# Where the rest tokens' transposed q stands in SyncE's queue, and four dummy matmuls less in the opening

## The chip, the cores and the metric

The kernel runs on one core of one Trainium2 chip. The metric is the device time of one execution in microseconds (us), lower is better. Eight runs of the kernel before took 285.57 to 286.43 us, with a median of 286.01 us.

## The reference

A linear attention is followed by a two-layer feed-forward network with a tanh gelu. The shapes are 8 batches, 8 heads, 576 tokens and 64 dimensions per head; the attention's result is read as 4608 tokens of 512 features, and the hidden layer has 2048.

```python
def phi(x):
    return np.where(x > 0, x, np.exp(x) - 1.0) + 1.0
q_p, k_p = phi(q), phi(k)
kv  = np.einsum('bhsd,bhse->bhde', k_p, v)
z   = np.sum(k_p, axis=2)
num = np.einsum('bhsd,bhde->bhse', q_p, kv)
den = np.einsum('bhsd,bhd->bhs', q_p, z)[..., None] + 1e-06
x   = (num / den).transpose(0, 2, 1, 3).reshape(B * S, H * D)
h   = x @ w_in
g   = 0.5 * h * (1 + tanh(sqrt(2/pi) * (h + 0.044715 * h**3)))
out = g @ w_out
```

## The kernel before, in words

**Tiling.** Of each batch's 576 tokens, 512 are its main part, in four chunks of 128. The last 64 of two batches together make one more tile of 128, the "rest" tile m of batches 2m and 2m+1. The network (`iteration(j)`, L736) is run for j = 0 to 7 on the 512 main tokens of batch j, and for j = 8 on the four rest tiles. An iteration is a list of steps that TensorE runs in order: 16 steps "h" (four matmuls of 128x512 each, L380, then a gelu on ScalarE, L390), and after them the steps "o" (four matmuls of 128x512 each, L720). After each step, `run(j, slot)` calls what was planned for this slot with `at(j, slot, fn, ...)` (L498): the preparation and the attention of the batches to come are written into these slots by hand. Each engine takes its instructions in the order in which they were written.

**The attention of a batch.** phi(x) is computed as min(exp(x), max(x + 1, 1)): the exponential on ScalarE (`exp_of`, L218), the linear part on VectorE (`linear_of`, L226), and the minimum on VectorE (`least_of`, L232). Then q's phi has to be transposed, so that it can be the weights of the matmuls with kv. From batch 2 on this is done by DMA transposes that SyncE issues: `least_q(b)` (L595) computes the minimum for q and issues one DMA transpose per chunk, for chunks 0, 1, 2 and 3 (L599). The rest tile has the same steps in `plan_rest(m)` (L668): its exponential at slot 15 of iteration m+2, and at slot 22 its linear part, its minimum and one DMA transpose into `qtr` (L673).

**Order around the change.** From batch 4 on, `plan_attention(b)` (L634) writes the attention of batch b into iteration j = b-1. At slot 4, that is after five h steps, `early` (L644) runs on TensorE 32 small matmuls with chunks 1 and 0 of the transposed q, then 16 with the rest tile's `qtr` (L282, m = b-4), and then the h steps go on. VectorE divides (L294, L295), and SyncE transposes the three results (L622, L649). At slot 22, `late` (L652) does chunks 2 and 3, the kv of the next batch (L248), and calls `least_q(b+1)`. In the same slot 22, after `late`, the `least` of `plan_rest` runs. So in SyncE's queue, in iterations 3 to 5, the four transposes of batch b+1's q come first and the transpose of the rest tile m = b-3 comes fifth; all five are used from slot 4 of the next iteration on, where the order of use is: chunks 1 and 0, the rest tile, and from slot 22 on chunks 2 and 3. In iteration 2, rest tile 0 has slot 22 to itself. SyncE's queue also carries all loads, and the transposes of the attention's results.

**The opening.** `first_batch` (L407) prepares batch 0. The function `keep_warm(n)` (L410) puts n matmuls of 128x512 on zeros into TensorE's queue, whose result nothing reads: 18 at the start, 10 after the first half of q is transposed on TensorE (L422), 7 after the second half, then one between the two groups of kv matmuls (L248). The first of these groups takes the first half of k and of v, the second takes the second half. v is cast to bf16 by VectorE in two halves (L237), k's phi is computed by VectorE just before. Each group's result is copied into `kvbd` by VectorE and ScalarE (L260), and the first matmuls with q follow (L353, L264).

Of the kernel before, what the change touches and what calls it, by code (L numbers as in the profile page):

```python
# [9 lines left out]
BF16 = mybir.dt.bfloat16  # L10
# [5 lines left out]
def kernel(  # L16
# [15 lines left out]
    nc = tc.nc  # L32
# [3 lines left out]
    P = 128  # L36
    HP = P // 2
    C = 4
    MAIN = P * C
    REST = S - MAIN  # L40
    NP = H // 2
# [12 lines left out]
    pt = ctx.enter_context(tc.tile_pool(name="pt", bufs=2))  # L54
# [3 lines left out]
    psm = ctx.enter_context(tc.tile_pool(name="psm", bufs=2))  # L58
# [17 lines left out]
    def bank(name, shape, dt=FP32):  # L76
        return ps_b.tile(shape, dt, name=name, tag="b")

    def pair_of_banks(name):
        return ps_a.tile([P, 2, 512], FP32, name=name, tag="a")  # L80
# [115 lines left out]
    phi, exps = {}, {}  # L196

    def maps_view(name, b, x, out, hs):


        i = x[:, hs].rearrange("p h (c d) -> p h c d", d=D)
        o = out[:, :, hs, :].rearrange("p c h d -> p h c d")
        if name == "qr" or (name == "q" and b > 1):
            i = i.rearrange("p (u a) c d -> p a u c d", a=2)
            o = o.rearrange("p (a u) c d -> p a u c d", a=2)
        return o, i

    def phi_tiles(name, b):
        n, hn = ld[name, b].shape[2] // D, ld[name, b].shape[1]
        phi[name, b] = pphi.tile([P, n, hn, D], BF16, name=name + "_p")  # L210

    def exp_of(name, b, hs=None):
        x = ld[name, b]
        hs = hs or slice(0, x.shape[1])
        if (name, b) not in exps:
            exps[name, b] = pe.tile([P, x.shape[2] // D, x.shape[1], D], BF16, name=name + "_e")
        o, i = maps_view(name, b, x, exps[name, b], hs)
        nc.scalar.activation(o, i, AF.Exp)  # L218

    def linear_of(name, b, hs=None):  # L220
        x = ld[name, b]
        hs = hs or slice(0, x.shape[1])
        if (name, b) not in phi:
            phi_tiles(name, b)
        o, i = maps_view(name, b, x, phi[name, b], hs)
        nc.vector.tensor_scalar(o, i, 1.0, 1.0, op0=ALU.add, op1=ALU.max)  # L226

    def least_of(name, b, hs=None):
        p, e = phi[name, b], exps[name, b]
        if hs:  # L230
            p, e = p[:, :, hs, :], e[:, :, hs, :]
        nc.vector.tensor_tensor(p, p, e, op=ALU.min)  # L232
# [69 lines left out]
    def x_tile():  # L302
        return px.tile([P, d_model], BF16, name="x")
# [72 lines left out]
    qts = {}  # L376
# [30 lines left out]
    def first_batch():  # L407
        w_ps = bank("w_ps", [P, 512])

        def keep_warm(n):  # L410
            for _ in range(n):
                nc.tensor.matmul(w_ps, lhsT=warm[:, 0:P], rhs=warm)  # L412

        qt = pt.tile([P, C, NP, P], BF16, name="qt")
        qs = (slice(0, 4), slice(4, 8))

        def transpose_q(s, fn):
            t_ps = bank("t_ps", [P, C, 2, P], BF16)
            for i in range(2):
                for c in range(C):  # L420
                    h = 4 * s + 2 * i
                    nc.tensor.transpose(  # L422
                        t_ps[:, c, i, :], phi["q", 0][:, c, h : h + 2, :], ident
                    )
            fn(out=qt[:, :, 2 * s : 2 * s + 2, :], in_=t_ps)

        keep_warm(18)
        for s in range(2):
            for n, hs in (("q", qs[s]), ("k", halves[s])):
                exp_of(n, 0, hs)  # L430
                linear_of(n, 0, hs)
                least_of(n, 0, hs)
        transpose_q(0, nc.scalar.copy)
        keep_warm(10)
        transpose_q(1, nc.scalar.copy)
        keep_warm(7)
        for ii in range(2):
            cast_v_paired(0, halves[ii], nc.vector.tensor_copy)
        kv_ps = [bank("kv_ps", [P, E]) for _ in range(2)]
        kv_paired(0, 0, lambda a, ii: kv_ps[a])  # L440
        for a, fn in enumerate((nc.vector.tensor_copy, nc.scalar.copy)):
            kv_evac(0, slice(2 * a, 2 * a + 1), kv_ps[a].rearrange("p (i e) -> p i e", i=1), fn)
        keep_warm(1)
        kv_ps = pair_of_banks("kv_ps")
        kv_paired(0, 1, lambda a, ii: kv_ps[:, a, 0:E])
        kv_evac(0, slice(1, 4, 2), kv_ps[:, :, 0:E], nc.vector.tensor_copy, nc.scalar.copy)
        for fs in (slice(0, 128), slice(128, 256), slice(256, 512)):
            cast_w_in(0, nc.gpsimd.tensor_copy, fs)
        cast_w_in(1, nc.gpsimd.tensor_copy, slice(256, 512))
        for i in range(2, 4):  # L450
            cast_w_in(i, nc.gpsimd.tensor_copy)
        for i in range(2):
            cast_w_out(i, nc.gpsimd.tensor_copy)

        xts[0] = pt.tile([P, NP, MAIN], BF16, name="xt")
        x = {0: x_tile()}

        def t(c, blocks=range(NP)):
            transpose_x(x[c], xt_chunk(0, c), nc.scalar.copy, blocks)

        def h(m, c, blocks=range(KM)):
            h_begin(0, m, slice(P * c, P * (c + 1)), blocks)

        first, second = range(2), range(2, 4)
        nab_half(x[0], qt[:, 0], 0)
        nab_half(x[0], qt[:, 0], 1)
        x[1] = nab(qt[:, 1], 0)
        t(0, first)
        h_begun[0][0] = bank("h_ps", [P, MAIN])
        nc.tensor.matmul(h_begun[0][0], lhsT=warm[:, 0:P], rhs=warm, skip_group_check=True)  # L470
        t(0, second)
        for m in range(2):
            h(m, 0, first)
        x[2] = nab_in_banks(qt[:, 2], 0)
        h(0, 0, second)
        t(1)
        h(1, 0, second)
        x[3] = nab(qt[:, 3], 0)
        cast_w_in(1, nc.vector.tensor_copy, slice(0, 256))
        h(2, 0)  # L480
        h(3, 0)
        t(2)
        for m in range(3):
            h(m, 1)
        t(3)
        gelu_table()
        h(3, 1)
        for c in (2, 3):
            for m in range(4):
                h(m, c)  # L490
# [7 lines left out]
    def at(j, slot, fn, *args):  # L498


        fill.setdefault((j, slot), []).append((fn, args))
# [90 lines left out]
        else:  # L592
            at(j, s + 2, least_of, "k", b)

    def least_q(b):  # L595
        least_of("q", b)
        qts[b] = pt.tile([P, C, NP, P], BF16, name="qt")
        for c in range(C):
            nc.sync.dma_start_transpose(  # L599
                out=qts[b][:, c],  # L600
                in_=phi["q", b][:, c].rearrange("p h d -> p (h d)"),
            )

    def kv_in_pair(b):
        kv_ps = pair_of_banks("kv_ps")
# [18 lines left out]
    rest_qt = {}  # L624
# [9 lines left out]
    def plan_attention(b):  # L634


        j, m = b - 1, b - 4

        def pair_of_chunks(c):
            in_banks = nab_quads_in_banks(qts[b][:, c + 1], (b, b))  # L640
            in_pair = nab_quads(qts[b][:, c], (b, b))
            return (c + 1, in_banks), (c, in_pair)

        def early():  # L644
            chunks = pair_of_chunks(0)
            rest = nab_quads_in_banks(rest_qt[m], (2 * m, 2 * m + 1))
            transposed_x(b, 1, chunks[0][1]())
            x = rest()
            nc.sync.dma_start_transpose(out=xt_rest[:, :, P * m : P * (m + 1)], in_=x)  # L649
            transposed_x(b, 0, chunks[1][1]())  # L650

        def late():  # L652
            chunks = pair_of_chunks(2)
            if b + 1 < B:
                kv_ps = [bank("kv_ps", [P, 2, E]) for _ in range(2)]
                for ii in range(2):
                    kv_paired(b + 1, ii, lambda a, ii: kv_ps[a][:, ii, :])
            for c, x_of in chunks:
                transposed_x(b, c, x_of())
            if b + 1 < B:  # L660
                for a in range(2):
                    nc.vector.tensor_copy(out=kvs[(b + 1) % 4][:, 2 * a : 2 * a + 2, :], in_=kv_ps[a])
                least_q(b + 1)

        at(j, 4, early)
        at(j, 22, late)

    def plan_rest(m):  # L668
        def least():
            linear_of("qr", m)  # L670
            least_of("qr", m)
            rest_qt[m] = psm.tile([P, NP, P], BF16, name="qtr")
            nc.sync.dma_start_transpose(  # L673
                out=rest_qt[m], in_=phi["qr", m][:, 0].rearrange("p h d -> p (h d)")
            )

        at(m + 2, 15, exp_of, "qr", m)
        at(m + 2, 22, least)

    def evac(dst, src, on_scalar):  # L680
        (nc.scalar.copy if on_scalar else nc.vector.tensor_copy)(dst, src)  # L681
# [105 lines left out]
    for b in range(4, B):  # L787
        plan_prepare(b, (b - 2, 13), (b - 2, 15))
        plan_attention(b)
        plan_rest(b - 4)  # L790
    for b in range(6, B):
        at(b - 3, 6, load_rest, b - 4)
        at(b - 3, 6, load_batch, b)
# [35 lines left out]
```

## Time and profile before

| quantity | value |
|---|---|
| median of 8 runs | 286.01 us (285.57 to 286.43) |
| the profiled execution, its own time | 285.72 us |
| its span, first to last instruction | 283.9 us, so 1.8 us lie outside |
| TensorE (PE) busy | 275.8 us, 97% |
| ScalarE (ACT) busy | 161.9 us, 57% |
| VectorE (DVE) busy | 106.0 us, 37% |
| weight loads (PEld) busy | 135.9 us, 48%, beside the matmuls |
| GpSimd (POOL) busy | 15.5 us, 5%, all before 43 us |
| 590 matmuls of L720, 551 of L380 | 126.2 us and 114.4 us |
| 35 recorded dummy matmuls of L412 (36 issued) | 10.6 us |
| DMA transposes of q by chunks (L599), issue to landing | 24, median 2.6 us |
| DMA transposes of a rest tile's q (L673), issue to landing | 4, 2.4 to 3.5 us |

All times inside the execution are in us from the start of the span. PE stands for a matmul on TensorE, PEld for a weight load, SPq for SyncE's queue of DMA issues, and L282 for line 282 of the code. In a timeline, a row has a start, the time from the start of its first to the end of its last instruction, the engine, the line, the operation with what it writes and reads, and how many instructions are merged into the row; in brackets stands how long the engine was idle before it, and for whom. Matmuls overlap one another: one of 128x512 has a length of 379 ns in the records, while the next begins 216 ns after it. So the time that work takes on TensorE is best read from start to start.

### The profile page before, as it was taken

The page shows a single profiled execution, that of the slowest core. Times are in us where ns is not written, and L with a number is a line of the kernel's source. Part 1 is how long each engine was busy: PE and PEld are TensorE (multiplying, and loading weights), DVE is VectorE, ACT ScalarE, POOL GpSimd, SP SyncE. Part 2 cuts the span into 40 slices and gives each one's busy share as a digit, 9 for nine tenths or more (in the row PEclk, how much of TensorE's full clock was granted, in tenths as well). Part 3 has the DMA queues.
Part 4 walks back from the last instruction along what each step waited for, and adds up shares of the span by engine and source line. Part 5 has one row for each costly group of instructions (what it writes and reads, how often), then busy time and mean ns, then how long its engine had stood idle before and what let it go on. Part 6 is the DMA issues. An engine that isn't in the chain of part 4 may idle for free.

```text
span 283.9 us, 5380 instructions
## 1 busy us (share of the span) xinstructions
PE 275.8 (97%) x2263; PEld 135.9 (48%) x2297; DVE 106.0 (37%) x193; ACT 161.9 (57%) x222; POOL 15.5 (5%) x22
## 2 busy tenths in 40 slices
PE   8999999999999999999999999999999999999995
PEld 3584455445454444445444544454444444444444
DVE  3850376344956342727080808081403000000001
ACT  4678878776966925693568445872650165027400
POOL 4147210000000000000000000000000000000000
PEclk9999999999999999999999999999999999999999
DMA  7999999968699868997539874015300510120022
GB/s 247 400 407 396 411 401 404 404 232 221 74 233 339 229 166 236 283 370 242 150 79 341 265 169 42 17 49 164 106 19 15 126 46 0 61 88 1 0 74 76
DMA packets 59591, 53.83 MB, mean 190 GB/s; under 512 B 35760, under 2 KB 45360, under 8 KB 59568
## 3 DMA queue, kind: packets, MB, share of 16 engines
q1 hardware_dynamic: 56784, 44.58, 52.9%
q10 hardware_dynamic: 2784, 8.91, 8.5%
q8 instruction: 18, 0.29, 0.4%
q14 instruction: 5, 0.04, 0.0%
HBM read 36.70 MB, written 9.44 MB: 163 GB/s over the span
## 4 chain that ended last, share of the span: by engine, by line
PE 94%; SPq 2%; DMA 1%; issue 1%; DVE 1%; ACT 0%
PE h_ps L380 42%; PE o_ps L720 42%; PE w_ps L412 4%; PE kv_ps L248 2%; SPq L599 2%; PE n_ps L282 1%; DMA qtr<-qr_p 1%; PE n_ps L264 1%; PE t_ps L372 1%; PE t_ps L526 0%; PE t_ps L422 0%; DVE x L362 0%; DVE kvbd L260 0%; DVE o_sb L681 0%; PE n_ps L353 0%
## 5 line engine op out<-in xcount | busy, mean ns | idle before, releaser
L720 PE MATMUL o_ps<-w_out_sb,g 128*128 128x512 bf16 (+2 forms) x590 | 126.2, 367 | 1.4 <-issue 0.6
L380 PE MATMUL h_ps<-xt,w_in_sb 128*128 128x512 bf16 (+1 forms) x551 | 114.4, 359 | 0.8 <-issue 0.2
L390 ACT ACTIVATE g<-h_ps 128x512 bf16<-128x512 f32 x144 | 84.9, 598 | 42.1 <-PE h_ps L380 40.3
L720 PEld LDWEIGHTS <-g 128*128 128x128 bf16 x608 | 57.4, 98 | 64.0
L380 PEld LDWEIGHTS <-w_in_sb 128*128 128x128 bf16 x628 | 57.9, 98 | 62.8
L681 ACT COPY o_sb<-o_ps 128x512 f32<-128x512 f32 (+1 forms) x19 | 10.8, 576 | 64.0 <-PE o_ps L720 62.4
L681 DVE COPY o_sb<-o_ps 128x512 f32<-128x512 f32 (+1 forms) x19 | 12.2, 648 | 72.4 <-PE o_ps L720 72.4
L295 DVE TENSOR_TENSOR x<-n_ps,r 128x256 bf16<-128x256 f32 (+1 forms) x49 | 26.4, 539 | 1.7
L294 DVE RECIPROCAL r<-n_ps 128x4 f32<-128x4 f32 (+1 forms) x49 | 9.2, 187 | 36.2 <-PE n_ps L282 26.6
L232 DVE TENSOR_TENSOR k_p<-k_p,k_e 128x2304 bf16<-128x2304 bf16 (+1 forms) x9 | 11.0, 1223 | 22.1 <-ACT k_e L218 21.8
L218 ACT ACTIVATE k_e<-k_x 128x2304 bf16<-128x2304 f32 (+1 forms) x9 | 17.1, 1903 | 0.8 <-DMA k_x<-in_k_dram 0.8
L218 ACT ACTIVATE q_e<-q_x 128x2048 bf16<-128x2048 f32 (+1 forms) x9 | 15.4, 1715 | 2.8 <-DMA q_x<-in_q_dram 2.8
L226 DVE TENSOR_SCALAR q_p<-q_x 128x2048 bf16<-128x2048 f32 (+1 forms) x9 | 9.9, 1103 | 13.2 <-DMA q_x<-in_q_dram 13.2
L232 DVE TENSOR_TENSOR q_p<-q_p,q_e 128x2048 bf16<-128x2048 bf16 (+1 forms) x9 | 9.9, 1102 | 11.5 <-ACT q_e L218 11.4
L380 PE MATMUL h_ps<-xt_rest,w_in_sb 128*128 128x512 bf16 x63 | 13.9, 379 | 0.1
L226 DVE TENSOR_SCALAR k_p<-k_x 128x2304 bf16<-128x2304 f32 (+1 forms) x9 | 11.0, 1220 | 4.2 <-DMA k_x<-in_k_dram 4.2
L412 PE MATMUL w_ps<-warm 128*128 128x512 bf16 x35 | 10.6, 454 | 1.2 <-DVE warm L181 1.2
L237 DVE CAST vp<-v_x 128x2304 bf16<-128x2304 f32 (+1 forms) x9 | 11.0, 1225 | 1.8 <-DMA v_x<-in_v_dram 1.6
L403 ACT ACT_TABLE_LOAD x8 | 10.3, 1283 | 0.1
L218 ACT ACT_TABLE_LOAD x7 | 9.0, 1283 | 0.1
L141 POOL CAST w_in_sb<-w_st 128x512 bf16<-128x512 f32 (+2 forms) x6 | 7.6, 1269 | 14.2 <-DMA w_st<-in_moe_w_in_dram 14.2
L412 PEld LDWEIGHTS <-warm 128*128 128x128 bf16 x36 | 3.9, 113 | 6.3 <-issue 2.9
(45 smaller groups left out, 77.2 us busy)
## 6 DMA issues: line engine op xcount, KB each, us to landing
out_dram<-o_sb ACTq DMA_DIRECT2D x16, 512.0 KB, 3.7
k_x<-in_k_dram SPq DMA_DIRECT2D x7, 1152.0 KB, 9.4
v_x<-in_v_dram SPq DMA_DIRECT2D x7, 1152.0 KB, 11.6
q_x<-in_q_dram SPq DMA_DIRECT2D x6, 1024.0 KB, 7.9
w_st<-in_moe_w_in_dram SPq DMA_DIRECT2D x3, 1024.0 KB, 13.4
q_x<-in_q_dram SPq DMA_DIRECT2D x4, 512.0 KB, 8.3
w_st<-in_moe_w_out_dram SPq DMA_DIRECT2D x2, 1024.0 KB, 12.5
w_st<-in_moe_w_out_dram SPq DMA_DIRECT2D x4, 512.0 KB, 11.2
```

The costliest lines, as they stand in the source:

```text
L218: nc.scalar.activation(o, i, AF.Exp)
L226: nc.vector.tensor_scalar(o, i, 1.0, 1.0, op0=ALU.add, op1=ALU.max)
L232: nc.vector.tensor_tensor(p, p, e, op=ALU.min)
L237: fn(out=vp_paired(b)[:, :, us, 0:D].rearrange("p j u d -> p u j d"), in_=ld["v", b][:, us].rearrange("p u (j d) -> p u j d", d=D),)
L294: nc.vector.reciprocal(r, n_v[heads + (D,)])
L295: nc.vector.tensor_tensor(x_v, n_v[heads + (slice(0, D),)], r[heads + (None,)].to_broadcast(shape + [D]), op=ALU.mult,)
L380: nc.tensor.matmul(h_ps[:, ts], lhsT=w_in_sb[:, c, P * m : P * (m + 1)], rhs=xt[:, c, ts], start=(c == 0), stop=(c == KM - 1), skip_group_ ...
L390: nc.scalar.activation(g[:, m, :], h_ps, AF.Gelu_apprx_tanh)
L403: nc.scalar.preload_act_table_set("gelu_apprx_tanh_and_others")
L412: nc.tensor.matmul(w_ps, lhsT=warm[:, 0:P], rhs=warm)
L681: (nc.scalar.copy if on_scalar else nc.vector.tensor_copy)(dst, src)
L720: nc.tensor.matmul(o_ps, lhsT=g[:, m, P * t : P * (t + 1)], rhs=w_out_sb[:, m, fs], start=(m == 0), stop=(m == MM - 1),)
```

## The change

Two things are changed.

In iterations 3 to 5, the rest tile's linear part, minimum and DMA transpose are called from inside `least_q`, between the transposes of q's chunks 0 and 1 and those of chunks 2 and 3. SyncE's queue then holds chunk 0, chunk 1, rest, chunk 2, chunk 3, where it held chunk 0, 1, 2, 3, rest. VectorE's order of instructions is what it was: q's minimum, then the rest tile's linear part and minimum. ScalarE's and GpSimd's orders are also the same, and so is the slot of everything. Iteration 2 keeps its rest tile 0 at slot 22.

In the opening, the dummy matmuls after the two transposes of q are 8 and 5, where they were 10 and 7.

```diff
         transpose_q(0, nc.scalar.copy)
-        keep_warm(10)
+        keep_warm(8)
         transpose_q(1, nc.scalar.copy)
-        keep_warm(7)
+        keep_warm(5)
...
-    def least_q(b):
-        least_of("q", b)
-        qts[b] = pt.tile([P, C, NP, P], BF16, name="qt")
-        for c in range(C):
+    def transposed_q(b, cs):
+        for c in cs:
             nc.sync.dma_start_transpose(
                 out=qts[b][:, c],
                 in_=phi["q", b][:, c].rearrange("p h d -> p (h d)"),
             )
+
+    def least_q(b, m=None):
+
+        least_of("q", b)
+        qts[b] = pt.tile([P, C, NP, P], BF16, name="qt")
+        transposed_q(b, (0, 1))
+        if m is not None:
+            least_rest(m)
+        transposed_q(b, (2, 3))
...
-                least_q(b + 1)
+                least_q(b + 1, b - 3)
...
-    def plan_rest(m):
-        def least():
-            linear_of("qr", m)
-            least_of("qr", m)
-            rest_qt[m] = psm.tile([P, NP, P], BF16, name="qtr")
-            nc.sync.dma_start_transpose(
-                out=rest_qt[m], in_=phi["qr", m][:, 0].rearrange("p h d -> p (h d)")
-            )
-
-        at(m + 2, 15, exp_of, "qr", m)
-        at(m + 2, 22, least)
+    def least_rest(m):
+        linear_of("qr", m)
+        least_of("qr", m)
+        rest_qt[m] = psm.tile([P, NP, P], BF16, name="qtr")
+        nc.sync.dma_start_transpose(
+            out=rest_qt[m], in_=phi["qr", m][:, 0].rearrange("p h d -> p (h d)")
+        )
...
     for b in range(4, B):
         plan_prepare(b, (b - 2, 13), (b - 2, 15))
         plan_attention(b)
-        plan_rest(b - 4)
+        at(b - 2, 15, exp_of, "qr", b - 4)
+    at(2, 22, least_rest, 0)
```

## The prediction

> **What bounds the kernel now.** I read the busy shares first and then the chain that ended last.
>
> ```profile
> PE 275.8 (97%) x2263; PEld 135.9 (48%) x2297; DVE 106.0 (37%) x193; ACT 161.9 (57%) x222; POOL 15.5 (5%) x22
> ...
> PE 94%; SPq 2%; DMA 1%; issue 1%; DVE 1%; ACT 0%
> ```
>
> TensorE is busy 97% of the span and carries 94% of the chain. So only two things can shorten this kernel: work taken off TensorE where nothing else is late, and a wait of TensorE that goes. The chain names one place where it leaves TensorE for SyncE's queue and a DMA. Told in order of time (start, length, what):
>
> ```profile
> 158.65 4.28 PE o_ps L720 x19
> 162.93 1.03 SPq L599
> ...
> 167.94 0.02 SPq L673
> ...
> 167.99 3.47 DMA qtr<-qr_p
> 171.46 0.04 issue
> 171.51 0.32 PE n_ps L282 x16
> ```
>
> Iteration 4 ends, SyncE issues q's four transposes one after the other, then the rest tile's; that one lands 3.47 us later, and TensorE's 16 matmuls with it start at 171.51. How much this costs I read not from the idle time in brackets, but from start to start, because matmuls overlap. TensorE's timeline at the four places where a rest tile is used:
>
> ```profile
> 111.58 0.45 PE L282 MATMUL n_ps<-kv,qt 64*64 64x65 bf16 x32
> 111.87 0.32 PE L282 MATMUL n_ps<-kvbd,qtr 64*64 64x65 bf16 x16
> ...
> 141.01 0.45 PE L282 MATMUL n_ps<-kv,qt 64*64 64x65 bf16 x32
> 141.47 0.32 PE L282 MATMUL n_ps<-kvbd,qtr 64*64 64x65 bf16 x16
> ...
> 170.62 0.45 PE L282 MATMUL n_ps<-kv,qt 64*64 64x65 bf16 x32
> 171.51 0.32 PE L282 MATMUL n_ps<-kv,qtr 64*64 64x65 bf16 x16 [0.44 <-DMA qtr<-qr_p]
> ...
> 200.65 0.45 PE L282 MATMUL n_ps<-kv,qt 64*64 64x65 bf16 x32
> 200.93 0.32 PE L282 MATMUL n_ps<-kv,qtr 64*64 64x65 bf16 x16
> ```
>
> From the 32 matmuls with q to the 16 with the rest tile it is 0.29 us at the first place and 0.28 us at the fourth, where nothing is waited for. At the third it is 0.89 us, so 0.61 us are lost. At the second it is 0.46 us, so 0.18 us are lost, though no bracket says so. The fourth is close: its transpose was issued at 197.86 and took 2.9 us, so it landed at about 200.76, some 0.14 us before its first weight load at 200.90.
>
> **Part one: the rest tile third in the queue instead of fifth.** It removes and adds no instruction. It moves one DMA transpose ahead of two others, in each of iterations 3 to 5. Two issues of q's transposes take about 2 x 1.26 = 2.5 us in SyncE's timeline (162.71 for the first, 5.18 us for all four), so at the third place the rest tile is issued at about 165.2 and, even with the same 3.5 us, lands at 168.7. The 16 matmuls could have begun at 170.90. That is 2.2 us to spare, and it covers the 0.61 us four times over. Its data is ready: VectorE ends the rest tile's minimum at 162.17 (161.74 + 0.43), before the first of q's transposes is issued at 162.71. So the transposes of chunks 2 and 3, which now stand behind it, wait for no VectorE either; they are one issue of 1.2 to 1.7 us later, and they are first used in slot 22, at 187.47, some 15 us after landing. Behind the five transposes stands the transpose of an attention result, which waits for VectorE's division (issued at 172.24) and doesn't move for this. What would be late next are chunks 1 and 0 of q, which TensorE needs at 170.62; they keep their places and were issued by 165.2, so they have over 2 us too. Gain: 0.61 + 0.18 = **0.79 us** in this execution. Bounds: in a run whose transposes land a little sooner, 0.2 us; in one where all three land 0.3 us later than here, about 1.5 us (0.91 + 0.48 + 0.16).
>
> The page DMA: Bandwidth & Descriptors of the Trainium skill, in Latency and other measured facts, gives DMA transposes 261 GB/s; for 128x512 values of 2 bytes I estimate 0.50 us each from it. By that figure, passing two transposes would be worth 1.0 us and not 2.5 us, which still covers the whole wait; the trace's rows (1.26 us per issue, 2.3 to 5.7 us to landing) disagree with it as a time per transpose, and they decide.
>
> **Part two: four dummies less.** A dummy costs 216 ns from start to start once TensorE is up to speed: the first of ten starts at 7.69, and what follows them at 9.85. Two fewer twice is 4 x 0.216 = 0.86 us of TensorE's queue. What counts is what waits for TensorE there:
>
> ```profile
> 9.85 0.61 PE L422 MATMUL t_ps<-ident,q_p 128*128 128x128 bf16 x8
> ...
> 10.76 0.76 DVE L237 CAST vp<-v_x 128x1152 bf16<-128x1152 f32 x1
> 11.63 0.76 DVE L237 CAST vp<-v_x 128x1152 bf16<-128x1152 f32 x1
> ...
> 11.90 0.48 PE L248 MATMUL kv_ps<-vp,k_p 64*64 64x65 bf16 x36
> 12.31 0.39 PE L412 MATMUL w_ps<-warm 128*128 128x512 bf16 x1
> 12.63 0.37 PEld L248 LDWEIGHTS <-k_p 64*64 64x64 bf16 x36 [0.23 <-issue]
> ...
> 13.18 0.29 DVE L260 CAST kvbd<-kv_ps 64x130 bf16<-64x130 f32 x1 [0.21 <-PE kv_ps L248]
> ```
>
> The second transposes could start 0.43 us sooner, at 9.42; VectorE has their input at 9.31 (8.62 + 0.69). The five dummies then end at about 11.05. The first kv group needs the first cast, done at 11.52, and can start at about 11.57 instead of 11.90; it takes 0.41 us, the one dummy after it 0.32 us to the next group, so TensorE would be ready for the second group at 12.30. But this one needs the second cast, done at 12.39: it starts at about 12.44 instead of 12.63. From here VectorE, which runs without a break from 7.83 to 12.39, is the bound, so 0.86 us of dummies bring **0.19 us**. The copies into `kvbd`, the first matmuls with q and the divisions follow in a chain and move with it. Is it kept? Things that do not move with TensorE have to be in time: the last quarter of the first part of w_in is cast on GpSimd by 15.45 and used after 16.24; batch 1's v is cast by 39.54 (38.18 + 1.36) and used at 39.87, the least spare I found, 0.33 us. So 0.19 us are kept. Bounds: 0 if a load is later than here, 0.86 us if TensorE and not VectorE is late in the opening.
>
> That last bound isn't idle. The dummies' weight loads are 0.43 us apart until 5.43 and 0.22 us from 5.73 on, although the granted clock reads 1.00 throughout: TensorE starts at half speed. The page TensorE: Matmul & The Clock Gate of the Trainium skill, Part 1, says that the clock opens after about 3.4 us of activity in a window that runs freely, so that the moment differs from run to run, and that an idle window of that length closes it. By that rule the sum above stands, or grows in a run that warms up later; no row of one trace can show the spread.
>
> **Sum.** 285.72 - 0.79 - 0.19 = 284.74 us for the profiled execution. It lies 0.29 us below the median of the runs shown, 286.01; taking the same 0.98 us off the median gives 285.0 us.
>
> **Rivals.**
> 1. *The opening gives nothing back*, because a load or VectorE holds the second kv group or a later cast. For it: the spare of 0.33 us at 39.87 is small. Against it: 0.19 fits in. Time: 286.01 - 0.79 = 285.2.
> 2. *The rest tile's wait was mostly this execution's.* For it: two of four places have no wait at all, and landing times range from 2.4 to 3.5 us. Against it: three of the four places lie within 0.2 us of a wait or in one, and the median run is slower than the profiled one. With 0.2 us from each part: 285.6.
> 3. *More than forecast*: TensorE warms up later in the usual run, so that the dummies are late there and removing them is worth up to 0.86 us. Time: 286.01 - 0.79 - 0.86 = 284.4.
> 4. *Slower*: the clock falls in the opening. Place: after the second dummies, TensorE now idles from 11.05 to 11.57, 0.52 us, and two idle stretches of about 0.4 us (before 13.81 and 14.82) follow. It decides from the point at which these add up to too little activity. Price: at the start the half speed lasted from 1.19 to 5.73, 4.5 us; as long a fall, in TensorE's work after 14 us, costs half of it, 2.3 us. Time: 286.01 - 0.79 + 2.3 = 287.5. Against it: with the two stretches of 0.4 us there now, the eight matmuls of 128x128 at 16.41 still take 0.45 us, 56 ns each, which is full speed.
>
> That the change doesn't do what it says is excluded: the order of the queues shows chunk 0, 1, rest, 2, 3 in iterations 3 to 5 and four dummies less.
>
> **How the numbers follow.** Forecast 0.52 (284.7 to 285.4), rival 1 0.15, rival 2 0.13, rival 3 0.11, rival 4 0.09. The range from 284.4 to 285.75 reaches over rivals 1 and 2 and to rival 3, and leaves out rival 4 and the edges of the others, below 2 in 10. About 0.2% (0.57 us) is what a measurement of this kernel can tell from no change, so faster means under 285.44: the forecast and rival 1 nearly whole, and rival 3, 0.75; the same is rival 2 and an edge of the forecast, 0.16; slower is rival 4, 0.09.
>
> **What would show it.** In the profile after: at all four places 0.28 to 0.29 us from the matmuls with q to those with the rest tile, and no SPq or qtr in the chain; the second kv group at about 12.4 and the copy into `kvbd` on VectorE at about 13.0; TensorE idle before the first kv group, with VectorE's cast named as its releaser; the matmuls at about 16.2 still 56 ns apart. It would be wrong if a wait stood in front of chunks 1 and 0 at slot 4, if matmuls of 128x128 after 13 us were 110 ns apart, or if TensorE waited for a cast near 39.7.

## The result, and the profile after

The changed kernel takes 284.71 us (median of 15 runs, 284.63 to 284.89). The kernel before, run beside it and before it, takes 285.71 us (median of 41 runs, 284.88 to 286.75). The ratio is 0.9964, with a 95% interval of 0.9955 to 0.9973: 0.36% faster, 1.0 us. Beside the median the spread changed: 0.26 us now, 1.87 us before.

The profiled execution took 284.64 us, with a span of 282.9 us. Its busy shares and the shares of its chain:

```profile
PE 274.9 (97%) x2260; PEld 135.7 (48%) x2293; DVE 105.9 (37%) x193; ACT 162.0 (57%) x222; POOL 15.5 (5%) x22
...
PE 93%; DMA 3%; issue 1%; SPq 1%; DVE 1%; ACT 0%
```

TensorE is busy for the same share as before. But the DMA in the chain is another one. Before, it was the rest tile's transpose at 168 us. Now it is the load of v's second half in the opening (chain in order of time: start, length, what):

```profile
3.36 8.18 DMA v_x<-in_v_dram
...
11.56 0.77 DVE vp L237
...
12.38 0.52 PE kv_ps L248 x33
```

The half lands at 11.54, VectorE casts it until 12.33, and only then TensorE's second kv group starts. The dummies, which stood here before, are gone from the chain. From here to the end the chain is TensorE, with a few short steps of VectorE and ScalarE in the opening and one at the end.

At the two places where TensorE had waited for the rest tile, the timeline now reads:

```profile
140.75 0.45 PE L282 MATMUL n_ps<-kv,qt 64*64 64x65 bf16 x32
141.03 0.32 PE L282 MATMUL n_ps<-kvbd,qtr 64*64 64x65 bf16 x16
...
170.18 0.45 PE L282 MATMUL n_ps<-kv,qt 64*64 64x65 bf16 x32
170.46 0.32 PE L282 MATMUL n_ps<-kv,qtr 64*64 64x65 bf16 x16
```

From start to start it is 0.28 us at both, as at the other two places (0.29 and 0.28). It was 0.46 and 0.89. So 0.18 + 0.61 = 0.79 us are gone. The queues around the second place (SPq is SyncE's, ACTq ScalarE's):

```profile
162.17 2.52 SPq L597 DMA_TRANSPOSE qt<-q_p  x2
164.78 1.22 SPq L679 DMA_TRANSPOSE qtr<-qr_p  x1
166.05 3.03 SPq L597 DMA_TRANSPOSE qt<-q_p  x2
166.58 0.39 ACTq L712 DMA_DIRECT2D out_dram<-o_sb  x1
```

The rest tile's transpose (L679, the old L673) stands third and landed 2.3 us after its issue, at 167.1, more than 3 us before it is needed. Note the last row: ScalarE issues a store of 512 KB 1.8 us after it. In the profile before, this store was issued 0.97 us *ahead* of the rest tile's transpose, which then took 3.5 us:

```profile
167.02 0.35 ACTq L709 DMA_DIRECT2D out_dram<-o_sb  x1
167.99 1.64 SPq L673 DMA_TRANSPOSE qtr<-qr_p  x1
```

This neighbour, which the prediction did not weigh, is what e4, e5 and e11 are about.

The opening:

```profile
10.69 1.63 DVE L237 CAST vp<-v_x 128x1152 bf16<-128x1152 f32 x2
11.50 0.37 PEld L248 LDWEIGHTS <-k_p 64*64 64x64 bf16 x36 [0.61 <-DVE vp L237]
...
12.38 0.48 PE L248 MATMUL kv_ps<-vp,k_p 64*64 64x65 bf16 x36 [0.40 <-DVE vp L237]
```

Both kv groups now wait for VectorE's cast, as the brackets say. The second starts 0.25 us sooner than before (12.63), and 0.07 us of this is not the change's: the loads came a little sooner, so that VectorE's second cast ends at 12.32 instead of 12.39. That leaves 0.18 us. The two terms add to 0.79 + 0.18 + 0.07 = 1.04 us, against 1.08 us between the two profiled executions (285.72 and 284.64).

### The profile page after: what moved, and what is told of

Its sections match the earlier page's. It is cut to its first block, busy times and chain, and to the rows that moved or that the text cites. A ratio compares the mean times of both kernels' runs of the same rounds, so it can differ in the third digit from the quotient of the medians.

```text
span 282.9 us, 5373 instructions
## 1 busy us (share of the span) xinstructions
PE 274.9 (97%) x2260; PEld 135.7 (48%) x2293; DVE 105.9 (37%) x193; ACT 162.0 (57%) x222; POOL 15.5 (5%) x22
## 4 chain that ended last, share of the span: by engine, by line
PE 93%; DMA 3%; issue 1%; SPq 1%; DVE 1%; ACT 0%
PE h_ps L380 44%; PE o_ps L723 44%; DMA v_x<-in_v_dram 3%; PE kv_ps L248 2%; PE n_ps L282 1%; PE n_ps L264 1%; PE t_ps L372 1%; SPq L92 1%; SPq L97 0%; PE t_ps L526 0%; DVE vp L237 0%; DVE x L362 0%; DVE kvbd L260 0%; DVE o_sb L684 0%; PE n_ps L353 0%
## 5 line engine op out<-in xcount | busy, mean ns | idle before, releaser
L412 PE MATMUL w_ps<-warm 128*128 128x512 bf16 x31 | 9.6, 474 | 1.2 <-DVE warm L181 1.2
L248 PE MATMUL kv_ps<-vp,k_p 64*64 64x65 bf16 x576 | 6.6, 194 | 0.5 <-DVE vp L237 0.4
## 6 DMA issues: line engine op xcount, KB each, us to landing
w_st<-in_moe_w_out_dram SPq DMA_DIRECT2D x2, 1024.0 KB, 12.5
```

Of the source, the lines that this page charges most:

```text
L248: nc.tensor.matmul(kv_of(a, ii)[HP * s : HP * (s + 1)], lhsT=kp[r, j, u, :], rhs=vp[r, j, u, :], start=(j == 0), stop=(j == J - 1), skip_g ...
```

## The experiments

Two theories stood against each other at first: that there are two gains, most of it from the rest tile's wait, or that most of it comes from the opening. Later the question became what makes the wait so long. Kernels e1 to e4 ran on one chip, e5 to e8 on a second, e9 to e12 on a third; each is compared with the kernel before on its own chip.

| kernel | median, us (lowest to highest) | before, there | ratio (95% interval) |
|---|---|---|---|
| e1 order alone, 10 and 7 dummies | 284.99 (284.66 to 285.56) | 285.86 | 0.9966 (0.9953 to 0.9979) |
| e2 dummies alone, old order | 285.64 (285.11 to 286.52) | 285.86 | 0.9993 (0.9979 to 1.0008) |
| e3 0 and 0 dummies | 285.75 (285.51 to 286.95) | 285.86 | 1.0003 (0.9987 to 1.0019) |
| e4 rest tile fourth | 284.97 (284.79 to 285.34) | 285.86 | 0.9970 (0.9956 to 0.9984) |
| e5 rest tile fifth, store later | 285.41 (284.71 to 286.77) | 286.18 | 0.9979 (0.9963 to 0.9995) |
| e6 4 and 2 dummies | 285.15 (284.65 to 286.70) | 286.18 | 0.9976 (0.9957 to 0.9994) |
| e7 v's cast shared | 284.69 (284.62 to 285.11) | 286.18 | 0.9951 (0.9931 to 0.9970) |
| e8 12 and 9 dummies | 286.07 (285.29 to 287.30) | 286.18 | 0.9997 (0.9981 to 1.0013) |
| e9 changed kernel | 284.80 (284.73 to 285.27) | 285.86 | 0.9962 (0.9946 to 0.9978) |
| e10 as e7 | 284.91 (284.70 to 285.05) | 285.86 | 0.9965 (0.9951 to 0.9978) |
| e11 as e5 | 285.61 (284.74 to 286.06) | 285.86 | 0.9988 (0.9976 to 1.0000) |
| e12 as e2 | 285.90 (285.59 to 286.19) | 285.86 | 0.9998 (0.9987 to 1.0009) |

### e1: the queue's order alone

```diff
-        keep_warm(8)
+        keep_warm(10)
         transpose_q(1, nc.scalar.copy)
-        keep_warm(5)
+        keep_warm(7)
```

> The queue's order of the changed kernel with the 10 and 7 dummy matmuls of the kernel before. Theory (two separate gains: 0.79 us from the rest tile's wait, the rest from the opening): no wait for the rest tile at any of the four places, 0.28 us from the matmuls with q to those with the rest tile, and a time between 284.8 and 285.3 us, some 0.2 to 0.5 us above the changed kernel's 284.71. Its times should still spread more than the changed kernel's 0.26 us, since the 35 dummies run ahead of the first kv group at a speed that depends on when TensorE gets faster. Rival (the waits were one execution's, and the opening brought most of it): about 285.5 us.

It is 0.87 us faster than the kernel before, and no place waits for the rest tile. The spread is 0.90 us. Its profiled execution was its slowest run, and shows why the dummies make a spread:

```profile
6.71 0.15 PEld L412 LDWEIGHTS <-warm 128*128 128x128 bf16 x1 [0.28 <-issue]
7.03 0.53 PEld L412 LDWEIGHTS <-warm 128*128 128x128 bf16 x3 [0.17 <-issue]
...
12.55 0.48 PE L248 MATMUL kv_ps<-vp,k_p 64*64 64x65 bf16 x36
...
13.28 0.48 PE L248 MATMUL kv_ps<-vp,k_p 64*64 64x65 bf16 x36
```

Weight loads of the dummies are 0.43 us apart until 6.71 here, and 0.22 us from 7.03 on; in the kernel before the change of speed came at 5.73. Each us that it comes later costs half a us of dummies: (7.03 - 5.73) / 2 = 0.65, and the second kv group starts 13.28 - 12.63 = 0.65 us later. Neither row of matmuls has a bracket: VectorE had ended its casts at 12.42, before both of them. So with 10 and 7 dummies the opening is bound by TensorE in such a run, and with 8 and 5 by v's cast. The median does not show what this is worth: e1's is 0.28 us above the changed kernel's 284.71 on another chip, but by the ratios to the kernel before (0.9966 and 0.9964) the two differ by 0.06 us, far less than the intervals.

### e2 and e12: the dummies alone

```diff
-        keep_warm(10)
+        keep_warm(8)
         transpose_q(1, nc.scalar.copy)
-        keep_warm(7)
+        keep_warm(5)
```

(on the kernel before)

> The 8 and 5 dummy matmuls of the changed kernel with the queue's order of the kernel before. Theory: the second kv group starts at about 12.4 us whenever TensorE gets faster, the waits for the rest tile remain at one to three places, and the time is 285.2 to 285.6 us, spread by 0.5 us or more, because the landing of the rest tile's transpose varies. Rival (opening brings most): 284.7 to 284.9 us with a small spread.

> The kernel of e2 (old order, 8 and 5 dummies), beside e9 and e11 on one chip: 0.8 to 1.0 us above e9, with waits for the rest tile of 0.2 to 0.8 us at two or three places.

Alone, the opening's part can't be told from no change: 0.22 us faster in e2, 0.04 us slower in e12. The waits for the rest tile are there, in e2's profile longer than in the one before:

```profile
141.02 0.45 PE L282 MATMUL n_ps<-kv,qt 64*64 64x65 bf16 x32
141.67 0.32 PE L282 MATMUL n_ps<-kvbd,qtr 64*64 64x65 bf16 x16 [0.20 <-DMA qtr<-qr_p]
...
170.81 0.45 PE L282 MATMUL n_ps<-kv,qt 64*64 64x65 bf16 x32
171.88 0.32 PE L282 MATMUL n_ps<-kv,qtr 64*64 64x65 bf16 x16 [0.62 <-DMA qtr<-qr_p]
```

With 0.28 us as the unhindered step, 0.37 and 0.79 us are lost, 1.16 us together; e12's profile has one such wait, 0.52 us, where two or three were expected. So the old order costs 0.5 to 1.2 us in the three profiles, different each time. The rival "the opening brought most" is refuted: e12 is 1.10 us above the changed kernel on the same chip (e9), a little more than the 0.8 to 1.0 expected, and the two differ in the queue's order alone.

Why does the opening's 0.18 us not show? In the profiles of e2 and e12 VectorE ends v's second cast at 12.60 and 12.86, where it was 12.39 before and 12.32 after. Over all profiles of this study that end lies between 12.32 and 12.86, apart from the two kernels that share this cast, because the first loads land at different times. In the nine profiles with 8 and 5 dummies or fewer and the cast unshared, v's second half lands between 11.54 and 12.08, and the second kv group starts 0.84 or 0.85 us after it each time: at 12.65 in e2 and 12.92 in e12, not at the 12.4 that was expected for any run. This moves the start of everything by more than the term that was forecast.

### e3 and e6: fewer dummies still

```diff
-        keep_warm(8)
+        keep_warm(0)          # e6: 4
         transpose_q(1, nc.scalar.copy)
-        keep_warm(5)
+        keep_warm(0)          # e6: 2
```

> The changed kernel without any dummy after the first and after the second transposes of q (0 and 0 instead of 8 and 5); the 18 at the start and the one between the kv groups stay. Theory of the opening (VectorE's cast of v's second half, and that half's arrival, are the bound): the first kv group starts at about 11.5 and the second at about 12.3 to 12.4, as in the changed kernel, so 284.7 us within 0.15. Rival 4 (the clock falls when too little runs): TensorE idles some 1.6 us before the second transposes and another 1.5 us after them, matmuls of 128x128 after 13 us begin 107 instead of 56 ns apart, and the time is 286 to 287.5 us.

> The changed kernel with 4 and 2 dummies instead of 8 and 5. TensorE idles about 0.8 us before the second transposes and 1.3 us before the first kv group, between the changed kernel (0.6 us in one place) and the one with none (1.8 and 1.7 us, clock halved from 12.5 to 15.4 us). Theory (the second kv group is bound by v's arrival and VectorE, and the clock falls only from longer idle stretches): 284.7 us within 0.15. Rival (the clock falls already): matmuls after 12.5 us at 107 instead of 56 ns per 128 columns, 285.3 to 286.5 us, in all or in some of the runs.

Without any, the clock falls in every run. The stretches of the opening (length, then busy time and count of each engine, granted clock, DMA share, GB/s):

```profile
9.00:12.50 3.50, 1.10 (x44) 0.91 (x46) 3.29 (x6) 3.01 (x4) 0.00 (x0) 0.96 1.05 397
12.50:15.50 3.00, 2.63 (x51) 2.14 (x52) 2.32 (x9) 0.84 (x3) 2.21 (x3) 0.50 1.08 401
```

TensorE was busy 1.10 of the 3.5 us from 9.0 (2.86 of 3.3 us in the changed kernel), and then ran at a granted clock of 0.50 from 12.5 to 15.5. The second kv group starts at 12.53, 0.84 us after v's second half lands, as with 8 and 5 dummies, so the theory was right there; but the small matmuls behind it take twice their time, and the span is 1.0 us longer. The twelve runs fall into groups by their mean granted clock. Seven with 0.993 or 0.994 take 285.5 to 285.8 us, one with 0.993 takes 286.2, and four with 0.987 or 0.988 take 286.6 to 287.0 us. Only these five are in the range that rival 4 was given, 286 to 287.5; the median, 285.75, lies below it. A mean of 0.994 over 283.9 us is 0.006 x 283.9 / 0.5 = 3.4 us at half speed, and 0.987 is 7.4 us: the clock falls for about 3.4 us, or for about twice that. The page TensorE: Matmul & The Clock Gate of the Trainium skill, Part 1, gives 3.4 us as the length of the window over which the activity is judged, and says that it runs freely; the lengths agree. It also says that an idle window closes the gate, and here TensorE was not idle but busy for about a third of the time; the measurement decides.

With 4 and 2 dummies the clock stays up in eight of twelve runs, 284.65 to 285.25 us, and falls in four: three at 286.6 to 286.7 us with 0.987, one at 285.98 with 0.993. So both theories are right in some runs. As far as these runs show, the limit lies between six and thirteen dummies, and the changed kernel stands on the safe side: none of its 21 runs here has a mean clock under 0.998.

### e8: more dummies

```diff
-        keep_warm(8)
+        keep_warm(12)
         transpose_q(1, nc.scalar.copy)
-        keep_warm(5)
+        keep_warm(9)
```

> The queue's order of the changed kernel with 12 and 9 dummies, four more than e1. Theory (with 10 and 7, TensorE's dummies are already later than v's cast in the usual run): the whole 4 x 0.216 = 0.86 us is added to e1, so 285.8 to 285.9 us, with a spread as wide as e1's 0.9 us. Rival (they are hidden): e1's 285.0 us.

The median is 286.07 us, 1.08 us above e1's on another chip; by the ratios it is 0.31% of 286 us, 0.89 us. Forecast were 0.86. This fits dummies that are paid for in full and take the queue's gain back; the two intervals together leave room for 0.3 to 1.5 us. The spread is 2.0 us. In its profile, which is its fastest run, the speed changed at 4.10, the second kv group starts at 12.99, and its row of matmuls has no bracket: v's cast had ended at 12.75.

### e4: the rest tile fourth

```diff
-        transposed_q(b, (0, 1))
+        transposed_q(b, (0, 1, 2))
         if m is not None:
             least_rest(m)
-        transposed_q(b, (2, 3))
+        transposed_q(b, (3,))
```

> The changed kernel with the rest tile fourth in the queue: chunk 0, 1, 2, rest, 3. Theory (passing one transpose is worth some 1.3 us, more than the 0.6 us that were missing): the rest tile is issued at about 166.1 us instead of 164.8 and lands some 0.7 us or more before TensorE needs it, so 284.7 to 284.8 us and no wait. Rival (by the page's 0.5 us per transpose, so that one place is not enough): a wait of about 0.1 us remains at one place, 284.8 to 285.0 us.

The theory missed. The issue came at 166.46, earlier than in the kernel before by 1.5 us, and yet:

```profile
162.53 3.84 SPq L597 DMA_TRANSPOSE qt<-q_p  x3
166.46 1.21 SPq L679 DMA_TRANSPOSE qtr<-qr_p  x1
166.95 0.39 ACTq L712 DMA_DIRECT2D out_dram<-o_sb  x1
...
170.54 0.45 PE L282 MATMUL n_ps<-kv,qt 64*64 64x65 bf16 x32
171.01 0.32 PE L282 MATMUL n_ps<-kv,qtr 64*64 64x65 bf16 x16
```

From start to start it is 0.47 us, so 0.19 us are lost here, and 0.05 us at the place before. The transpose was issued 0.49 us ahead of the store and landed 4.5 us later; one place further ahead, in the changed kernel, it took 2.3 us. So a place in the queue is not worth a fixed 1.3 us. The rival's time came, with a wait of about its size, but not for its reason: the place did bring 1.5 us at the issue, and the landing took them back. What decides here seems to be how far behind it the store is issued: in e4 it came 0.5 to 0.9 us behind, and the transposes took 3.9 to 4.8 us; in the eight profiles with the rest tile third it came 1.7 to 2.4 us behind at this place and the next, and all sixteen took 2.3 or 2.4 us. It is not the only thing that stretches one: at the place before, at 134.81, the changed kernel's transpose also took 3.8 us to land, with the store 2.3 us behind it, and six of the eight took 3.3 to 4.0 us there, the other two (e7, e8) 2.3 us. Why is not settled; it had enough to spare each time.

### e5 and e11: the rest tile fifth again, the store later

```diff
             if j == 0:
                 at(1, 2, store)
+            elif t == C - 1:
+                at(j + 1, 10, store)
             else:
                 store()
```

(on e2)

> The queue's order of the kernel before (rest tile fifth) and 8 and 5 dummies, as in e2, with one change: from iteration 1 on, the store of the second half of an iteration's output (512 KB, issued by ScalarE beside the rest tile's transpose) is issued at slot 10 of the next iteration. Theory (it is this store on the same DMA engines that makes the rest tile's transpose take 3.5 to 4.5 us, and a transpose ahead of it takes 2.4): the rest tile, still fifth, lands 2.3 to 2.6 us after its issue, no wait is left at any of the four places, and the time is that of the changed kernel, 284.6 to 284.9 us. Rival (the place in the queue alone counts, since transposes go one after the other): landing stays at 3 us or more, the waits of 0.2 to 0.8 us stay, 285.3 to 285.7 us.

> The kernel of e5, beside e9 and e12 on one chip: old order, 8 and 5 dummies, and the 512 KB store moved to slot 10. The part of the queue's gain that comes from the store is (e12 - e11) / (e12 - e9). Theory: the larger part, 0.5 to 0.7 us of about 0.9; the rest of it (0.2 to 0.4) is the place in the queue, since in fifth place the transpose has only 0.6 us to spare and any delay of the four before it becomes a wait. Rival: e11 is within 0.2 us of e12, then the store is not the cause.

The mechanism is shown by e11's profile, whose answer for the rest tile's four transposes, all still last in their group, is

```profile
DMA to landing us min/median/max: 2.3/2.3/2.4
```

where it is 2.4/3.0/3.5 in e12, the same kernel with the store in its old place. In iterations 3 to 5, where the store was moved away from the transpose, all six transposes of e5 and e11 took 2.3 us; the nine in the old order with the store in place (before, e2, e12) took 2.6 to 4.2 us. In iteration 2 no store is issued within 2 us in any order; there e5's transpose took 3.4 us and all others 2.4, and why is open. No place waits for the rest tile in either profile of e5 and e11. But the time is not that of the changed kernel: e5's profiled run, 284.89 us, is within what was expected, its median, 285.41, is not. Of the 1.10 us between e12 and e9, e11 gives 0.29 us, not the 0.5 to 0.7 that were expected. e11's profile shows a new wait, at the start of the next iteration (first its place in the chain, then the row of the timeline):

```profile
160.00 7.03 DMA xt<-x
```

```profile
167.16 4.48 PE L380 MATMUL h_ps<-xt,w_in_sb 128*128 128x512 bf16 x19 [1.08 <-DMA xt<-x]
```

The store now goes out at 146.92, just ahead of the loads of the next batch, and the transpose of an attention result that is issued at 160.00 takes 7.0 us, instead of up to 4.5 at this place in the two profiles of the changed kernel. The load of v lands later too, at 164.1 (150.05 + 14.0) against 161.4 in e9 (149.05 + 12.3). That the moved store is what makes this wait is likely and not shown; e5's profile has the same store there, and this transpose took 5.8 us without a wait. How much of the old order's cost is the store's, in time, is therefore not settled; that the store is what stretches the rest tile's transpose in fifth place is.

### e7, e10 and e9: is there more in the opening?

```diff
-        for ii in range(2):
-            cast_v_paired(0, halves[ii], nc.vector.tensor_copy)
+        cast_v_paired(0, halves[0], nc.vector.tensor_copy)
+        dst = vp_paired(0)[:, :, halves[1], 0:D].rearrange("p j u d -> p u j d")
+        src = ld["v", 0][:, halves[1]].rearrange("p u (j d) -> p u j d", d=D)
+        nc.vector.tensor_copy(out=dst[:, :, 0:6], in_=src[:, :, 0:6])
+        nc.scalar.copy(out=dst[:, :, 6:J], in_=src[:, :, 6:J])
```

> The changed kernel, with the cast of v's second half in the opening shared: six of the nine j on VectorE, three on ScalarE, which is idle then. If this cast (0.76 us after the half's arrival at about 11.5) is what the second kv group waits for, VectorE ends 0.25 us sooner, ScalarE ends its part at 12.2 or so, and the group starts at about 12.25 (then bound by the dummy between the groups) instead of 12.38: 0.1 to 0.15 us faster than the changed kernel, 284.55 to 284.65 us. If the group is bound elsewhere: 284.7 us or slower.

> The kernel of e7 (cast of v's second half shared with ScalarE), beside the changed kernel on one chip. Theory (the second kv group started 12.25 instead of 12.38, and the first copies into kvbd sooner): 0.1 us faster than e9. Rival: within 0.05 us of e9, since other moments of the opening vary by more.

> The changed kernel itself, on the same chip as the next three, so that small differences can be compared. 284.7 us with a spread under 0.5 us if it is as steady as before; on a chip where the kernel before takes longer, up to 284.9.

In e7's profile the second group starts at 12.25, as expected. Its median is 284.69 us, where 284.55 to 284.65 were expected, and its fastest runs take 284.62. In e10, beside the changed kernel on one chip, the median is 0.11 us above it; the first cast in e10's profile starts at 11.02, against 10.81 in e9's, so the loads came later. If there is a gain of 0.1 us, it is smaller than what the arrival of the loads moves from run to run. The changed kernel itself spreads by 0.54 us in e9, a little more than the 0.5 expected. No version here is measurably faster than it.

## Why the prediction was right, and where it was off

The forecast was 285.0 us from a median of 286.01, so 0.98 us less. Measured are 1.00 us between the medians. The level is 0.3 us lower because the median of the kernel before fell from 286.01 (8 runs) to 285.71 (41 runs): the profiled execution, with 285.72, turned out to be a usual one. Against it the forecast was 284.74, and the profiled execution after took 284.64. That 0.98 and 1.00 agree so closely is partly luck: the wait was 0.52 and 1.16 us in two other profiles of the old order, and the opening's part moved the median by 0.22 us in e2 and by -0.04 us in e12.

**The rest tile, 0.79 us: right.** Both waits are gone to the hundredth, and what they cost was rightly read from start to start: the bracket showed 0.44 us where 0.61 were lost, and none where 0.18 were lost. Over many runs the term is 0.87 us (e1 against the kernel before) and 1.10 us (e12 against e9), inside the bounds of 0.2 to 1.5 us; so rival 2, that the wait was mostly this execution's, is refuted. **Its reason was half right.** The step "passing two transposes is worth 2 x 1.26 us" holds for the issue (164.78 against the 165.2 worked out). But the landing was taken as the same 3.5 us, as though that were the transpose's own time. At the place that matters most it took 2.3 us in third place, 4.5 in fourth (e4), and 2.3 in fifth with the store out of the way (e11). The step failed safely: it only made the spare larger. It would have misled anyone who used it to choose the fourth place.

**What would be late next: right.** Chunks 1 and 0 did not wait in any profile with the rest tile third, and chunks 2 and 3 stayed hidden.

**The opening, 0.19 us: right in the profile, not measurable alone.** The second kv group followed v's cast by 0.06 us, as worked out (12.32 and 12.38), and the brackets name VectorE in both groups. But the step "VectorE, which runs without a break from 7.83 to 12.39, is the bound" is half right. VectorE waited for a load: in the profile before, v's second half was issued at 3.36 and landed 8.2 us later, at about 11.6, and its cast started at 11.63; in the profile after it landed at 11.54, and the cast started at 11.56. So the load sets the moment, and the cast is the last step behind it. TensorE's own times were also off: its second transposes started at 9.70 and not at 9.42, mostly because it got faster at 6.23 instead of 5.73, and the wait for the cast took this up. In the runs of e2 and e12 the term is lost in the arrival of the loads, so the medians alone don't exclude rival 1, that the opening gives nothing back. The case for the larger value, up to 0.86 us when TensorE gets faster later, is also in the runs: e1's slowest execution started the second group 0.65 us later than the kernel before. It is not the usual run: e1's median is only 0.28 us above the changed kernel's, on another chip. So rival 3, 284.4 us, did not come.

**Rival 4, the falling clock: did not happen, and is real.** The forecast put its price at 2.3 us. The runs of e3 and e6 in which it fell, on other chips, are 0.8 to 2.2 us above the changed kernel's 284.7 to 284.8, with half the granted clock for 3.4 or 7 us. Removing four dummies of 36 is safe here, removing eleven is not.

**What was not foreseen** is the spread. As far as the profiles show, the kernel before varies for two reasons beside the arrival of the loads: the length of the rest tile's transpose beside the store, and the moment at which TensorE gets faster. The change takes TensorE off both, and its 15 runs lie within 0.26 us (six more on another chip, e9, within 0.54).

## What to carry to other kernels

Put transfers into a queue in the order in which their results are used, and look at what other queues issue at the same time: here a transpose issued 1.7 us or more ahead of a large store landed in time at every place, and one issued 0.5 to 0.9 us ahead of it (e4) was late at two of three. Read the cost of a wait from start to start against a place of the same code that doesn't wait, not from the idle time in brackets. Dummy work that keeps a clock up is hidden only while something else is later, here a load; take as much of it away as brings that other thing into the chain, and test the step beyond, since the clock's fall comes in some runs first.

## What the runs showed of the hardware

- **A DMA transpose beside a store.** The rest tile's transpose of 128x512 values took 2.3 us to land in e5 and e11, in iterations 3 to 5, where no store was near, and 2.6 to 4.8 us where it was issued within 1.1 us of a 512 KB store by ScalarE (before, e2, e4 and e12; 3.9 to 4.8 us in e4, where the store came 0.5 to 0.9 us behind it). The issue on SyncE took 1.2 us in these rows of e5 and e11, 1.45 to 1.70 us in the nine rows behind a store, and 1.2, 1.2 and 2.7 us in e4. A store is not the only cause: 3.3 to 4.0 us came up seven times with none issued within 1.7 us.
- **The moment at which TensorE gets faster.** In fourteen profiles the dummies' weight loads went from 0.43 to 0.22 us apart at 4.1 to 7.1 us after the span's start, with the same dummies from 1.19 on. The granted clock reads 1.00 in this stretch all the same. The page TensorE: Matmul & The Clock Gate, Part 1, gives a window of 3.4 us that runs freely, so that the moment varies; the range of 3.0 us found here agrees with that, but not with the 500 ns to either side that the page gives for the variation.
